# Two square roots, an exponential table, a clock and eighteen row numbers in an attention and experts kernel

## The chip, the cores and the metric

The kernel is one launch on one core of a Trainium2 chip. Its time is the device time of that launch in microseconds (us), the median of several runs. The engines are TensorE (PE in the profile, PEld for its weight loads), VectorE (DVE), ScalarE (ACT), GpSimd (POOL) and SyncE (SP, which here only issues DMAs).

## The reference

Three layers follow each other in fp32. Nothing is returned but the last.

```python
B, H, S, D = 4, 8, 576, 64
scores = where(block_i >= block_j, q @ k.T / 8, -1e9)     # blocks of 64 rows
attn = exp(scores - max); attn /= sum + 1e-9
x = (attn @ v) as rows                                    # 2304 x 512
xn = x / (norm(x) + 1e-6);  en = emb / (norm(emb) + 1e-6) # 8 experts
logits = xn @ en.T / tau                                  # tau = 0.1
expert = argmax(logits); gate = softmax(logits)[expert]
y = gate * (relu(x @ w1[expert]) @ w2[expert])            # 512 -> 1024 -> 512
h = y @ w_in;  out = (h * sigmoid(h)) @ w_out             # 512 -> 2048 -> 512
```

## The kernel before

**Stages.** Attention goes over 16 pairs (a batch and two heads each). For a pair, ScalarE or VectorE splits k and q into a high and a low part (`split`, L656), TensorE makes scores in three products (`s`), VectorE takes each row's maximum (`mx`), ScalarE makes the exponentials and their sums (`p`), TensorE transposes them (`pt`) and multiplies with v (`o`). A last small product with `rmat` turns `o` into rows of x and, in the same matmul, into the logits, for which `rmat` holds the normed expert rows (`experts`, L691, and `expert_rows`, L709). The scores of one pair come in three units: `full`, which takes both score buffers in PSUM, and two more that need a buffer back, that is, the exponentials before them. While attention runs, pieces of `w_in` are converted (`conv`, tiles `wbits`, `wcv`).

Then rows are sorted by expert into slots of 128 (`_Route`). 6 slots are filled from the first three batches (`early`), the others after the last batch (`late`, `rest`). `gates` (L1249) computes the softmax weight of each row from its logits and from `nr`, its norm, which is the root of the sum of squares `ss`. Each slot s is gathered, transposed (`xt`), multiplied by w1 (`h`), put through relu, transposed (`ht`), multiplied by w2 (`y`) and scaled by `gate` (`yout`, L1471). The last layer runs in 6 chunks of 3 slots: transposes `yt`, `up` (products `g`, then sigmoid) and `down` (products `o` into three PSUM accumulators), and `store` (L1550), which copies an accumulator out and scatters its 128 rows to `out` by an indirect DMA on GpSimd. The first chunks take their row numbers from `tokg`, the later ones read them back from DRAM with the rows (`yi`).

**Roots before.** L700 takes the root of the experts' 8 sums of squares on ScalarE; L702 is an exponential whose value nobody uses, placed behind it so that the exponential's table is loaded again. L1258 takes the root of 128x18 sums of squares on ScalarE, L1263 an exponential after it. ScalarE holds one table at a time; the instruction ACT_TABLE_LOAD changes it.

**Order of the work.** Everything between L1743 and the end is recorded in a list (`_Plan`) and put in order by a list scheduler with costs and latencies of its own. Each engine executes its instructions in the order that comes out. Work that two engines can do (copies, relus, splits) goes to the one that would finish it first by the plan (`bind`, L375), so a change of an instruction can move others. The plan takes 1283 ns for a change of table (L425) and 107 ns and more for transposes and fp32 products. The build is done four times (`_best`, L1808), each time with the due times of the one before, and the shortest plan is kept. `gates` is recorded with a priority of -1000, ahead of what stands around it. The identity matrix (L1736, L1737) is made ahead of the plan.

**Store before.** Its recorded call issues two instructions on GpSimd, a copy of 128 row numbers into a tile of their own and the scatter that reads them:

```python
eng.tensor_copy(ix, st["i"][:, a:a + 1])
ins = eng.indirect_dma_start(out, IndirectOffsetOnAxis(ap=ix, axis=0), o, None)
```

Of the kernel before, what the change touches and what calls it, by code (L numbers as in the profile page):

```python
# [9 lines left out]
F32 = mybir.dt.float32  # L10
F32R = mybir.dt.float32r
BF16 = mybir.dt.bfloat16
I32 = mybir.dt.int32
U32 = mybir.dt.uint32
AF = mybir.ActivationFunctionType
ALU = mybir.AluOpType
# [3 lines left out]
P = 128  # L20
# [8 lines left out]
NT = NTOK // P  # L29
# [8 lines left out]
PRE = 1  # L38
# [16 lines left out]
CH = 3  # L55
# [2 lines left out]
EXP_HI = 122879.9921875  # L58
NEG = -2.0 ** 100
STAY, STAY_NS, CHANGE = 30, 2000.0, 190.0  # L60
ROUNDS = 3
SQS = 100
WL = 2500.0
# [477 lines left out]
        self.free = dict.fromkeys(self.ENGINES, t)  # L541


def _column(b, tl):


    if tl == 4:
        return NC1 - 1 if b < 2 else NT - 1
    return 4 * b + tl + (b == 3)
# [52 lines left out]
def _attention(first, ctx, late, tc, plan, q, k, v, emb, tau, x_dram, identr, lr_all, ss_all, conv=None):  # L602


    nc = plan
    ident = identr.bitcast(F32)

    def pool(name, bufs, ctx=late, **kw):
        side = "left" if ctx is first else "right"
        return plan.pool(ctx.enter_context(tc.tile_pool(name=name, bufs=bufs, side=side, **kw)),  # L610
                         bufs)
# [6 lines left out]
    cp = pool("a_const", 1)  # L618
    vp = pool("a_v", 3)
    wk = pool("a_wk", 2)  # L620
    sm = pool("a_sm", 4)
    ps_t = pool("ps_t", 3, space=PSUM)
    ps_o = pool("ps_o", 1, space=PSUM)
    sp = pool("a_split", 3, ctx)
# [45 lines left out]
    load(0, "k")  # L670
    load(0, "q")


    maskq = cp.tile([P, P], F32R, name="maskq")
    maskk = cp.tile([P, 64], F32R, name="maskk")
# [15 lines left out]
    def experts():  # L691

        em = wk.tile([E, DM], F32, tag="ot", name="em")
        nc.sync.dma_start(em, emb)
        ta = cp.tile([E, 1], F32, name="ta")
        nc.sync.dma_start(ta, tau.partition_broadcast(E))
        esq = wk.tile([E, DM], F32, tag="ot", name="esq")
        en_s = cp.tile([E, 5], F32, name="en_s")
        nc.scalar.activation(esq, em, AF.Square, accum_out=en_s[:, 0:1])
        nc.scalar.activation(en_s[:, 1:2], en_s[:, 0:1], AF.Sqrt)  # L700
        if PRE:
            nc.scalar.activation(en_s[:, 4:5], en_s[:, 1:2], AF.Exp, scale=0.0)  # L702
        nc.vector.tensor_scalar(en_s[:, 2:3], en_s[:, 1:2], 1e-6, ta, ALU.add, ALU.mult)
        nc.vector.reciprocal(en_s[:, 3:4], en_s[:, 2:3])
        nc.vector.tensor_scalar_mul(esq, em, en_s[:, 3:4])
        nc.gpsimd.memset(rmat, 0.0)
        return esq
# [263 lines left out]
    for i in range(-2, NP + 2):  # L971
# [14 lines left out]
        st = s_units(i + 1) if 0 <= i + 1 < NP else []  # L986
# [15 lines left out]
class _Route:  # L1002
# [59 lines left out]
    @staticmethod  # L1062
    def bc(ap, axis, shape):
        return ap.unsqueeze(axis).to_broadcast(shape)
# [184 lines left out]
    def gates(self, pool, psum):  # L1249

        self.part = 4
        nc, V, bc = self.nc, self.nc.vector, self.bc
        self.choose(pool, NC1, NT)

        T8 = [P, NT, E]
        nr, gt = (self.tile(pool, x, [P, NT]) for x in ("nr", "gt"))
        pr = self.tile(pool, "pr", T8)
        nc.scalar.activation(nr, self.ss, AF.Sqrt)  # L1258
        V.tensor_scalar(nr, nr, 1e-6, None, ALU.add)
        V.reciprocal(nr, nr)  # L1260
        V.tensor_tensor(pr, self.lr, bc(self.mx, 2, T8), ALU.subtract)
        V.tensor_tensor(pr, pr, bc(nr, 2, T8), ALU.mult)
        nc.scalar.activation(pr, pr, AF.Exp)  # L1263
        V.tensor_reduce(gt, pr, AX.X, ALU.add)
        V.tensor_scalar(gt, gt, 1e-9, None, ALU.add)
        V.reciprocal(gt, gt)

        g3 = self.tile(pool, "g3", [P, NT, 3], BF16)
        for a in range(3):
            V.tensor_copy(g3[:, :, a], gt)  # L1270
            if a < 2:
                V.tensor_tensor(gt, gt, g3[:, :, a], ALU.subtract)
        self.g3 = g3
        self.places_of(pool, psum, "g1", self.first, NC1, 0)
# [12 lines left out]
def _layers(ctx, stage, early, scores, late, tc, plan, w1, w2, x_dram, y_dram, out, ident, route, xgs, conv, right):  # L1287

    nc = plan
# [194 lines left out]
    def chunk(c):  # L1484
        CW = CH * P
        st = {}

        def rows():
            st["y"] = yrows(c)
            if c < NC:  # L1490
                st["i"] = tokg[:, CH * c:CH * c + CH]
                return
            r0 = CW * (c - NC)
            nc.sync.dma_start(
                st["y"], y_dram[r0:r0 + CW, :].rearrange("(a p) d -> p a d", p=P))
            st["i"] = chp.tile([P, CH], I32, tag="yi", name=f"yi_{c}", bufs=2)
            nc.vector.tensor_copy(st["i"], st["y"][:, :, DM])

        def trans(kc):
            if kc == 0:  # L1500
                st["t"] = chp.tile([P, 2, KC, CW], F32R, tag="yt", name=f"yt_{c}")
            pt = psum(f"yt{kc}_{c}", "t" if c > YT else "c")
            for a in range(CH):
                nc.tensor.transpose(pt[:, a * P:(a + 1) * P],
                                    st["y"][:, a, kc * P:(kc + 1) * P], ident)
            nc.copy(st["t"][:, 0, kc], pt[:, 0:CW])
            nc.sub(st["t"][:, 1, kc], pt[:, 0:CW],
                                 st["t"][:, 0, kc].bitcast(F32))

        W = {}  # L1510

        def parts(w, f):
            if (w, f) not in W:
                if c == 0:
                    conv.piece(16 * w + f)
                W[w, f] = split((conv.win[:, f], conv.wout[:, f:f + 1, :])[w], f"w{w}_{c}_{f}")

        def up(f):
            parts(0, f)
            hi, lo = W.pop((0, f))  # L1520
            pt = psum(f"g{f}_{c}", "c")[:, 0:CW]
            t = st["t"]
            for kc in range(KC):
                nc.tensor.matmul(pt, hi[:, kc], t[:, 0, kc], start=(kc == 0), stop=False)
                nc.tensor.matmul(pt, hi[:, kc], t[:, 1, kc], start=False, stop=False)
                nc.tensor.matmul(pt, lo[:, kc], t[:, 0, kc], start=False, stop=(kc == KC - 1))
            sg = wk.tile([P, CW], F32, tag="sg", name=f"sg{f}_{c}")
            nc.scalar.activation(sg, pt, AF.Sigmoid)
            nc.vector.tensor_tensor(sg, pt, sg, ALU.mult)
            g = wk.tile([P, 2, CW], F32R, tag="g", name=f"g{f}_{c}")  # L1530
            nc.copy(g[:, 0], sg)
            nc.sub(g[:, 1], sg, g[:, 0].bitcast(F32))
            st["g", f] = g

        def down(*fs):
            if fs[0] == 0:
                st["o"] = [ps["a"].tile([P, DM], F32, tag="acc", name=f"o{a}_{c}")
                           for a in range(CH)]
            w = {}
            for f in fs:  # L1540
                parts(1, f)
                w[f] = *W.pop((1, f)), st.pop(("g", f))
            for a in range(CH):
                r = slice(a * P, a * P + P)
                for f in fs:
                    hi, lo, g = w[f]
                    three(st["o"][a], g[:, 0, r], g[:, 1, r], hi[:, 0], lo[:, 0],
                          f == 0, f == FC2 - 1)

        def store(a):  # L1550
            o = wk.tile([P, DM], F32, tag="o", name=f"os{a}_{c}", bufs=CH)
            nc.copy(o, st["o"][a])
            ix = wk.tile([P, 1], I32, tag="ix", name=f"ix{a}_{c}", bufs=CH)

            def f(eng):


                eng.tensor_copy(ix, st["i"][:, a:a + 1])  # L1558
                ins = eng.indirect_dma_start(out, IndirectOffsetOnAxis(ap=ix, axis=0), o, None)  # L1559
                for old in stores:  # L1560
                    tc.declare_no_dep(ins.ins, old.ins, reason="other rows")
                stores.append(ins)

            plan.call({"gpsimd": (f, 728.0)}, [plan._box(o), plan._box(st["i"])],
                      [plan._box(ix), (f"out_{c}_{a}", 0, 1, ((0, 1),))], dma=True)

        head = [(0.0, rows, [])] + [(0.35, lambda kc=kc: trans(kc), []) for kc in range(KC)]
        u = []
        order = [(up, 0)] + [x for f in range(1, FC2) for x in ((up, f), (down, f - 1))] + [
            (down, FC2 - 1)]  # L1570
        if c == nch - 1:

            order[-4:] = [(up, FC2 - 1), (down, FC2 - 3), (down, FC2 - 2, FC2 - 1)]
        for f, *n in order:
            u.append((1.95 * len(n), lambda f=f, n=n: f(*n),
                      [lambda f=f, m=m: parts(int(f is down), m) for m in n]))
        u += [(0.0, lambda a=a: store(a), []) for a in range(CH)]
        return head, u

# [92 lines left out]
    wk = pool("m_wk", 2)  # L1672
# [5 lines left out]
    for c in range(nch):  # L1678
# [3 lines left out]
        for at, units in ((HA, head[1:]), (HR, head[:1])):  # L1682
            i = max(n - at, 0)
            seq_c[i:i] = units
        seq_c += body
    a, c, due = early, 0, -DUE
    while a < len(seq_s) or c < len(seq_c):

        if c < len(seq_c) and a >= need[seq_c[c][0]] and (
                due <= 0 or c <= KC or a >= len(seq_s)):  # L1690
            _, w, f, _ = seq_c[c]
            c += 1
            due += w
        else:
# [4 lines left out]
            w, f = seq_s[a]  # L1699
# [108 lines left out]
def _best(build):  # L1808

    nc, plan = build(None)  # L1810
    last = plan
    for _ in range(ROUNDS):
        found, last = build(last.latest())
# [32 lines left out]
```

## Time and profile before

| what | value |
|---|---|
| median of 3 runs | 891.82 us (891.19 to 893.75) |
| the profiled execution: time of the run, span in the trace | 892.14 us, 890.4 us |
| PE, DVE, ACT, POOL busy, share of the span | 96%, 81%, 62%, 14% |
| mean granted clock of TensorE | 0.994 |
| ACT_TABLE_LOAD in the whole trace | 6, of 1283 ns |

The time of a run is 1.74 us more than the span, which goes from the first to the last instruction on the core. A busy PE is not a PE at its peak. Idle time of an engine counts only where another one waits for it.

### The profile page before, as it was taken

Reading aid. Unit: us, or ns where it says so; the run is one execution under the profiler, and the core shown is the slowest. Engines: PE = TensorE matmul, PEld = TensorE weight load, DVE = VectorE, ACT = ScalarE, POOL = GpSimd, SP = SyncE. Lnnn points to the kernel's source line nnn. Section 1 sums busy time; section 2 is a strip of 40 time slices with the busy share of each in tenths; the row PEclk is TensorE's granted clock in tenths of the full one; section 3 lists DMA queues with packets and bytes.
Section 4 is the critical chain, followed back from the end, with each engine's and each line's share of the span. In section 5 each row is a group of like instructions: output and inputs, shape, how many; then the busy total and the mean of one; then the engine's idle time right before and its main releaser. Section 6 shows DMA issues by size and latency. Waiting matters only on the chain.

```text
span 890.4 us, 13848 instructions
## 1 busy us (share of the span) xinstructions
PE 856.0 (96%) x4986; PEld 713.9 (80%) x4986; DVE 722.6 (81%) x1264; ACT 554.1 (62%) x1128; POOL 121.9 (14%) x162
## 2 busy tenths in 40 slices
PE   5999999999999999999999999999999999999995
PEld 4777677766567888888888888888999999999994
DVE  6989798988999799999888888887677767667672
ACT  7889787976467588888866665665334235334332
POOL 3013131123310000211311111002001001001001
PEclk9999999999999999999999999999999999999998
DMA  6545362473044477530102230342002002000000
GB/s 191 164 122 165 111 180 82 122 256 82 13 159 140 140 272 272 178 94 26 71 24 76 68 119 24 107 132 72 34 1 71 1 1 72 1 0 36 1 1 35
DMA packets 38440, 82.75 MB, mean 93 GB/s; under 512 B 5208, under 2 KB 13400, under 8 KB 38368
## 3 DMA queue, kind: packets, MB, share of 16 engines
q1 hardware_dynamic: 32736, 63.47, 22.2%
q0 software_dynamic: 5632, 18.36, 6.7%
q8 instruction: 40, 0.66, 0.3%
q14 instruction: 32, 0.26, 0.1%
HBM read 123.23 MB, written 13.11 MB: 153 GB/s over the span
## 4 chain that ended last, share of the span: by engine, by line
PE 65%; POOL 0%; POOLq 0%; issue 0%; ACT 0%
PE o L199 22%; PE g L199 22%; PE y L199 9%; PE h L199 9%; PE ht L199 2%; PE xt L199 1%; PE yt L199 1%; POOL out_dram L1559 0%; POOLq L1838 0%; ACT os L199 0%; POOL ix L1558 0%; POOLq L1559 0%
## 5 line engine op out<-in xcount | busy, mean ns | idle before, releaser
L199 PE MATMUL o<-w,g 128*128 128x512 f32 x864 | 234.2, 396 | 0.0
L199 PE MATMUL g<-yt,w 128*128 128x384 f32 x1152 | 230.7, 337 | 0.0
L199 PEld LDWEIGHTS g<-yt,w 128*128 128x128 f32 x1152 | 203.9, 188 | 13.8
L199 PEld LDWEIGHTS o<-w,g 128*128 128x128 f32 x864 | 160.0, 188 | 27.4 <-ACT g L199 0.3
L199 ACT ACTIVATE sg<-g 128x384 f32<-128x384 f32 x96 | 47.4, 494 | 141.9 <-PE g L199 141.8
L199 PE MATMUL y<-w2s,ht 128*128 128x512 f32 x450 | 131.3, 402 | 1.2 <-DVE w2s L199 1.2
L199 PE MATMUL h<-w1s,xt 128*128 128x512 f32 x450 | 110.4, 394 | 3.4 <-DVE xt L199 2.0
L199 PEld LDWEIGHTS h<-w1s,xt 128*128 128x128 f32 x450 | 83.5, 188 | 22.1 <-ACT h L199 2.0
L199 DVE TENSOR_TENSOR w1s<-wraw,w1s 128x1024 fp32r<-128x1024 f32 x75 | 91.2, 1221 | 11.4 <-ACT w1s L199 11.1
L199 DVE TENSOR_TENSOR w2s<-wraw,w2s 128x1024 fp32r<-128x1024 f32 x75 | 91.0, 1224 | 10.0 <-ACT w2s L199 8.7
L199 PEld LDWEIGHTS y<-w2s,ht 128*128 128x128 f32 x450 | 81.2, 188 | 16.3 <-DVE w2s L199 2.7
L199 ACT ACTIVATE p<-s,mx 128x576 f32<-128x576 f32 (+4 forms) x160 | 82.7, 527 | 15.7 <-DVE mx L199 12.9
L199 DVE TENSOR_TENSOR w<-win,w 128x512 fp32r<-128x512 f32 x96 | 66.0, 689 | 24.0 <-ACT w L199 23.4
L199 ACT CAST w2s<-wraw 128x1024 fp32r<-128x1024 f32 x68 | 71.0, 1051 | 14.2 <-PE h L199 7.4
L199 ACT CAST g<-sg 128x384 fp32r<-128x384 f32 x96 | 49.4, 514 | 39.9 <-DVE sg L199 38.3
L258 PE MATMUL s<-ks,qs 64*128 64x288 f32 (+4 forms) x576 | 61.3, 344 | 13.1 <-ACT p L199 7.7
L199 DVE TENSOR_REDUCE mx<-s 128x1 f32<-128x576 f32 (+3 forms) x96 | 64.6, 705 | 10.5 <-PE s L258 9.5
L199 ACT CAST w1s<-wraw 128x1024 fp32r<-128x1024 f32 x53 | 55.6, 1054 | 20.7 <-PE y L199 15.2
L199 DVE TENSOR_TENSOR w<-wout,w 128x512 fp32r<-128x512 f32 x96 | 65.6, 683 | 0.2 <-ACT w L199 0.2
L199 ACT CAST w<-win 128x512 fp32r<-128x512 f32 x75 | 46.6, 625 | 28.7 <-PE o L199 28.6
L258 PEld LDWEIGHTS s<-ks,qs 64*128 64x128 f32 x576 | 46.5, 199 | 20.0 <-ACT p L199 10.5
L199 DVE TENSOR_TENSOR sg<-g,sg 128x384 f32<-128x384 f32 x96 | 53.3, 556 | 10.6 <-ACT sg L199 7.9
(194 smaller groups left out, 1127.5 us busy)
## 6 DMA issues: line engine op xcount, KB each, us to landing
wraw<-in_moe_w_dram SPq DMA_DIRECT2D x76, 1024.0 KB
wbits<-in_moe_w_in_dram SPq DMA_DIRECT2D x16, 512.0 KB
wbits<-in_moe_w_out_dram SPq DMA_DIRECT2D x16, 512.0 KB
k<-in_k_dram SPq DMA_DIRECT2D x16, 288.0 KB
q<-in_q_dram SPq DMA_DIRECT2D x16, 288.0 KB
v<-in_v_dram SPq DMA_DIRECT2D x16, 256.0 KB
x_rows<-xe POOLq DMA_DIRECT2D x16, 256.0 KB, 4.1
wraw<-in_moe_w_dram SPq DMA_DIRECT2D x8, 512.0 KB
```

Source lines behind the costliest of these rows:

```text
L199: alts = {e: (lambda eng, m=m, a=a, k=k: getattr(eng, m)(*a, **k), self._cost(e, m, a, k), self._shares(e, m, a, k) if e != "tensor" else ...
L258: eng.matmul(out, a, b, **kw)
```

## The change

The root on ScalarE is replaced at both places by a start value from the bits of the number (a shift and an addition) and three steps of Heron on VectorE, each a reciprocal and two scalar_tensor_tensor operations; the steps leave twice the root, and a factor of 0.5 goes into the addition of 1e-6. The exponential at L702 goes. A new exponential of one column of zeros and 14 fp32 products of the identity with itself, whose result nobody reads, stand behind the loads of the first k and q. The copies of row numbers are recorded at the start of a chunk's `down` work, each into its own tile, and the call of a store issues the scatter and behind it a copy of the row numbers into a tile that nobody reads.

```diff
+GROOT, WARM = 1, 14
+def _root(V, z, t, x):
+    zi, xi = z.bitcast(I32), x.bitcast(I32)
+    V.tensor_scalar(zi, xi, 1, None, ALU.logical_shift_right)
+    V.tensor_scalar(zi, zi, float(0x20400000), None, ALU.add)
+    for _ in range(3):
+        V.reciprocal(t, z)
+        V.scalar_tensor_tensor(t, t, 2.0, x, ALU.mult, ALU.mult)
+        V.scalar_tensor_tensor(z, z, 0.5, t, ALU.mult, ALU.add)
...
     load(0, "k")
     load(0, "q")
+    one = cp.tile([P, 1], F32, name="one")
+    nc.vector.memset(one, 0.0)
+    nc.scalar.activation(one, one, AF.Exp)
+    pt = ps_t.tile([P, 512], F32, tag="t", name="t_warm")
+    for _ in range(WARM):
+        nc.tensor.matmul(pt[:, 0:P], ident, ident, start=True, stop=True)
...
-        nc.scalar.activation(en_s[:, 1:2], en_s[:, 0:1], AF.Sqrt)
-        if PRE:
-            nc.scalar.activation(en_s[:, 4:5], en_s[:, 1:2], AF.Exp, scale=0.0)
-        nc.vector.tensor_scalar(en_s[:, 2:3], en_s[:, 1:2], 1e-6, ta, ALU.add, ALU.mult)
+        _root(nc.vector, en_s[:, 1:2], en_s[:, 4:5], en_s[:, 0:1])
+        nc.vector.tensor_scalar(en_s[:, 2:3], en_s[:, 1:2], 0.5, 1e-6, ALU.mult, ALU.add)
+        nc.vector.tensor_tensor(en_s[:, 2:3], en_s[:, 2:3], ta, ALU.mult)
...
-        nc.scalar.activation(nr, self.ss, AF.Sqrt)
-        V.tensor_scalar(nr, nr, 1e-6, None, ALU.add)
+        if GROOT:
+            _root(V, nr, nt, self.ss)
+            V.tensor_scalar(nr, nr, 0.5, 1e-6, ALU.mult, ALU.add)
...
             if fs[0] == 0:
+                st["ix"] = [wk.tile([P, 1], I32, tag="ix", name=f"ix{a}_{c}", bufs=CH)
+                            for a in range(CH)]
+                for a in range(CH):
+                    nc.gpsimd.tensor_copy(st["ix"][a], st["i"][:, a:a + 1])
...
-                eng.tensor_copy(ix, st["i"][:, a:a + 1])
                 ins = eng.indirect_dma_start(out, IndirectOffsetOnAxis(ap=ix, axis=0), o, None)
...
+                eng.tensor_copy(spare, ix)
```

## Rows read from the trace of the kernel before

**Rows 1.** Windows: stretch, length, busy of PE, PEld, DVE, ACT, POOL, clock, DMA, GB/s.

```profile
10.00:15.00 5.00, 4.08 (x30) 3.80 (x30) 2.14 (x6) 4.32 (x10) 2.19 (x8) 1.00 0.56 170
...
40.00:60.00 20.00, 19.92 (x195) 15.84 (x192) 18.37 (x42) 15.74 (x46) 2.40 (x2) 1.00 0.37 112
...
220.00:240.00 20.00, 17.86 (x81) 11.26 (x80) 18.65 (x55) 8.39 (x13) 2.93 (x2) 1.00 0.05 14
...
270.00:280.00 10.00, 10.00 (x52) 8.55 (x51) 9.76 (x15) 9.12 (x13) 0.00 (x0) 1.00 0.46 159
```

**Rows 2.** Timeline, ACT to 11 us: start, length, engine, instruction, idle before.

```profile
0.81 1.28 ACT L199 ACT_TABLE_LOAD   x1 [0.81 <-PEq L1832]
...
6.45 0.67 ACT L199 CAST ks<-k 128x576 fp32r<-128x576 f32 x1 [0.62 <-DMA k<-in_k_dram]
...
7.14 1.28 ACT L199 ACT_TABLE_LOAD   x1
...
8.66 1.28 ACT L199 ACT_TABLE_LOAD   x1
...
10.06 0.72 ACT L199 ACTIVATE p<-s,mx 128x576 f32<-128x576 f32 x1
```

**Rows 3.** Timeline, DVE and PE of the same stretch.

```profile
1.42 0.65 DVE L1737 CAST ident<-xg 128x128 fp32r<-128x128 f32 x1 [1.42 <-POOL xg masks.py:199]
...
5.27 1.33 PE L258 MATMUL s<-ks,qs 64*128 64x288 f32 x8 [5.27 <-ACT qs L199]
...
6.47 0.83 PE L258 MATMUL s<-ks,qs 64*128 64x288 f32 x4
...
7.46 0.46 DVE L199 TENSOR_SCALAR qs<-q 128x576 fp32r<-128x576 f32 x1 [1.40 <-DMA q<-in_q_dram]
...
8.51 1.42 DVE L199 TENSOR_REDUCE mx<-s 128x1 f32<-128x576 f32 x2
...
10.92 1.12 PE L258 MATMUL s<-ks,qs 64*128 64x448 f32 x4 [3.63 <-ACT p L199]
```

**Rows 4.** Timeline of PE at three later places, and one window.

```profile
18.80 1.09 PE L199 MATMUL pt<-ident,p 128*128 128x128 f32 x4 [0.25 <-DVE pt L199]
...
29.69 1.53 PE L199 MATMUL pt<-ident,p 128*128 128x128 f32 x12
...
188.26 0.67 PE L258 MATMUL s<-ks,qs 64*128 64x448 f32 x4 [1.41 <-ACT p L199]
```

**Rows 5.** Window of PE: stretch, length, busy, clock, DMA, GB/s.

```profile
188.00:192.00 4.00, 3.74 (x45) 0.77 0.74 278
```

**Rows 6.** Timeline around the gates.

```profile
214.40 0.22 ACT L199 ACTIVATE r_nr<-ss 128x18 f32<-128x18 f32 x1
...
218.62 3.01 PE L199 MATMUL h<-w1s,xt 128*128 128x512 f32 x12 [1.79 <-DVE xt L199]
219.59 0.17 DVE L199 TENSOR_SCALAR r_nr<-r_nr 128x18 f32<-128x18 f32 x1
...
222.68 0.30 DVE L199 TENSOR_REDUCE r_gt<-r_pr 128x18 f32<-128x144 f32 x1
...
224.02 0.17 DVE L199 TENSOR_SCALAR r_gt<-r_gt 128x18 f32<-128x18 f32 x1
224.10 0.17 DVE L199 TENSOR_SCALAR c_cnt<-r_run 128x8 f32<-128x8 f32 x1
...
227.92 0.18 DVE L199 CAST r_g<-r_gt 128x18 bf16<-128x18 f32 x1
...
231.93 0.16 DVE L199 TENSOR_TENSOR gate<-gate,g 128x6 f32<-128x6 f32 x1
```

**Rows 7.** Timeline of POOL at the end.

```profile
880.70 0.98 POOL L1559 DMA_INDIRECT out_dram<-os,ix  x1 [60.04 <-ACT os L199]
881.69 0.19 POOL L1558 COPY ix<-yi 128x1 int32<-128x1 int32 x1
882.16 0.98 POOL L1559 DMA_INDIRECT out_dram<-os,ix  x1 [0.28 <-POOL ix L1558]
```

More of the change, by code (lines that the diff above doesn't have):

```diff
@@ L1255, in gates @@
         T8 = [P, NT, E]
-        nr, gt = (self.tile(pool, x, [P, NT]) for x in ("nr", "gt"))
+        nr, gt, nt = (self.tile(pool, x, [P, NT]) for x in ("nr", "gt", "nt"))
         pr = self.tile(pool, "pr", T8)
-        nc.scalar.activation(nr, self.ss, AF.Sqrt)
-        V.tensor_scalar(nr, nr, 1e-6, None, ALU.add)
+        if GROOT:
+            _root(V, nr, nt, self.ss)
+            V.tensor_scalar(nr, nr, 0.5, 1e-6, ALU.mult, ALU.add)
+        else:
+            nc.scalar.activation(nr, self.ss, AF.Sqrt)
+            V.tensor_scalar(nr, nr, 1e-6, None, ALU.add)
         V.reciprocal(nr, nr)
@@ L1552, in store @@
             nc.copy(o, st["o"][a])
-            ix = wk.tile([P, 1], I32, tag="ix", name=f"ix{a}_{c}", bufs=CH)
+            ix = st["ix"][a]
+            spare = wk.tile([P, 1], I32, tag="spare", name=f"sp{a}_{c}", bufs=CH)
             def f(eng):
-                eng.tensor_copy(ix, st["i"][:, a:a + 1])
                 ins = eng.indirect_dma_start(out, IndirectOffsetOnAxis(ap=ix, axis=0), o, None)
@@ L1562, in f @@
                 stores.append(ins)
-            plan.call({"gpsimd": (f, 728.0)}, [plan._box(o), plan._box(st["i"])],
-                      [plan._box(ix), (f"out_{c}_{a}", 0, 1, ((0, 1),))], dma=True)
+                eng.tensor_copy(spare, ix)
+            plan.call({"gpsimd": (f, 728.0)}, [plan._box(o), plan._box(ix)],
+                      [plan._box(spare), (f"out_{c}_{a}", 0, 1, ((0, 1),))], dma=True)
         head = [(0.0, rows, [])] + [(0.35, lambda kc=kc: trans(kc), []) for kc in range(KC)]
```

## The prediction

> **What bounds the kernel now.** I read the windows first. PE is busy 19.92 of 20 us at 40 to 60 and all of 270 to 280, while VectorE stands at 18.37 of 20 and 9.76 of 10 [rows 1]. So the body is bound by TensorE with VectorE close behind; a delay of either reaches the end there, and time taken from ScalarE reaches it only where somebody waits for ScalarE. The windows name the exceptions. From 10 to 15 us PE has 4.08 of 5 us, and at 220 to 240 it has 17.86 of 20 while VectorE has 18.65 and ScalarE only 8.39 [rows 1]. Three places matter for this change, and for each I read the timeline.
>
> At the start PE finishes the first scores at 6.47 + 0.83 = 7.30 and then sits idle 3.63 us until 10.92, released by ScalarE's first `p` [rows 3]. ScalarE ends `ks` at 6.45 + 0.67 = 7.12, loads a table at 7.14, another at 8.66, and starts `p` at 10.06 [rows 2]: 2.94 us that hold two loads of 1.28 and two tiny activations. But `p` also needs a row maximum. The two `mx` began only at 8.51, since VectorE first did the q split of the next pair, for which it had waited 1.40 us on a DMA [rows 3]. One reduction is 1.42 / 2 = 0.71, so the first was there at 9.22.
>
> Around the gates, the products `h` at 218.62 waited 1.79 us for VectorE's `xt` split [rows 6]. ScalarE's root, at 214.40, was long done, and VectorE came to its result only at 219.59 [rows 6].
>
> At the end POOL alone sets the pace: scatter 0.98 at 880.70, copy at 881.69, 0.28 of waiting, scatter at 882.16 [rows 7]. The next copy and scatter repeat this; nothing else runs.
>
> **The change part by part.** The sum is made against the profiled execution, 892.14 us, which is a span of 890.4 and 1.74 around it. The median of the three runs is 891.82, 0.32 lower.
>
> *The start.* Gone are two loads, a root and a dummy exponential, 2.94 us of ScalarE ahead of the first `p`. The new exponential's load takes the place of the load at 0.81 [rows 2], which lies ahead of the arrival of k, so it costs nothing; uncovered it would cost 1.28. What is late next is `mx`. If VectorE keeps its order, `p` starts about 0.1 behind 9.22: a gain of 10.06 - 9.35 = 0.7. If the scheduler, which no longer sees two loads of 1283 ns between the scores and `p`, puts `mx` first, then VectorE was idle (the 1.40 before 7.46) and `mx` starts some 0.2 after the scores end, at 7.5; `p` follows at 7.5 + 0.71 + 0.1 = 8.3, a gain of 1.75. I take 1.75: the reduction is then the only thing between two products on the engine that bounds everything, and the split serves a later pair. Ends: 2.94 gained at best. On the other side about 14 new VectorE operations for the experts' root come in here. The nearest, on 18 columns, starts 0.08 behind its predecessor and lasts 0.17 [rows 6]; 14 x 0.17 = 2.4 if all stood in front of `mx`, of which 1.40 finds VectorE idle, so a loss of 1.0 less the 0.7: 0.3 lost at worst. The next engine downstream is PE, nearly full from here on, so the gain is carried on to the end.
>
> *The 14 products.* The trace has no fp32 product of the identity; the nearest rows are transposes of the same shape, 4 in 1.09 us at 18.80 and 12 in 1.53 at 29.69 [rows 4], 0.27 and 0.13 each: the lower and the upper of the two clock levels (1.2 and 2.4 GHz), though no granted clock below 1.00 is recorded there. The identity is ready at 1.42 + 0.65 = 2.07 [rows 3]. 14 of them end between 2.07 + 1.8 = 3.9 and 2.07 + 3.8 = 5.9; the scores began at 5.27. So they cost 0 to 0.6, and if the clock is then up, the 12 score products save up to half of their 2.03 us, 1.0. I take zero, since the low parts of q are not there before about 6.1 anyway. Does the higher level last until the second scores? A later stretch says no: after PE had idled 1.41 us at 188.26 [rows 4], the granted clock of 188 to 192 averages 0.77 [rows 5], that is, part of it stood at the lower level. The gap here will be about 2 us. The Trainium skill says the same of idle stretches in "TensorE: Matmul & The Clock Gate", under "What's actually happening", and it is the rule that speaks against this edit; the fourth case below is what happens if it is wrong here.
>
> *The gates.* Gone are two loads and a root, 2.78 us of ScalarE, in a stretch where ScalarE idles more than half [rows 1]: nothing by itself. Added are 11 small operations on VectorE (13 for root and addition of 1e-6 and the reciprocal, where 2 were). They lie beside large ones; 224.02 and 224.10 start 0.08 apart [rows 6], so I take 0.1 each, 1.1 us, in a stretch that VectorE bounds. Against it stands that a relu or a cast of 0.7 to 1.0 may go to the freed ScalarE. I take a net loss of 0.4. Ends: 11 x 0.17 plus waiting of 0.06 each, 2.5 lost; two casts moved, 1.5 gained. By the Trainium skill, "VectorE: DVE Perf Modes", "The DRAIN you can't avoid", the next operation does not start until the pipe is empty, which would make it 11 x 0.17 = 1.9 lost and the sum 1.5 worse in that term; the two starts 0.08 apart speak against it here.
>
> *The stores.* The copies move to the start of `down`, where POOL, busy for 14% of the span, hides them; behind them in POOL's queue are only gathers and scatters of rows that are planned ahead. The first scatter waited 60.04 us on ScalarE, not on its copy [rows 7], so nothing is gained there. The second and third lose the wait of 0.28 but keep a copy of 0.19 before them, the one into `spare`. 2 x 0.28 = 0.56. Ends: 0 if the 0.28 is what an indirect DMA needs to start, 0.94 if the copy is overlapped too. I take 0.5.
>
> *Everything else.* No DMA is added or moved past another, but the scheduler lays the whole order anew. I put nothing for that, with an estimated 1.5 us to either side: PE's idle time at 220 to 240 alone is 2.14 us [rows 1], and a new order may find or lose about that.
>
> Sum: -1.75 + 0.4 - 0.5 = -1.85, 890.3 by the profiled execution's own time and 890.0 against the median. I predict 889.9.
>
> **The rivals.** *Order at the start unchanged.* VectorE still does the next pair's split before `mx`: -0.7, and the gates cost their full 1.1, the stores give 0.3. Sum +0.1: 891.9. For it: that split was also ahead when nothing forced it. Against: it was ahead while 2.57 us of loads covered it.
>
> *The gate comes late (slower).* The root is a chain of 11 links, and each has to wait for the one before it while large operations are let in between. The seven links from 222.68 to 227.92 took 5.24 us, 0.75 each [rows 6]. 11 x 0.75 = 8.2 us; before, 219.59 - 214.62 = 5.0 us lay between the end of the root on ScalarE and the addition. The gate, at 231.93, would come 3.2 us later, and if larger operations of 1.2 us slip between the links, 6. Slot 0's PSUM bank is held until it is scaled, so PE stalls for what goes beyond about half a microsecond of slack. It decides from a gate later than about 234.5: 6 - 0.5 = 5.5 lost, less 2.2 from start and stores: 895.1. Against it: the chain can start 5 us earlier than the addition did, in slots that exist already.
>
> *The clock stays up.* If the level reached by the 14 products outlasts the gap, the products from 10.92 to about 22 run at twice the rate. PE was busy 4.08 of 5 us there [rows 1], so some 9 of 11 us, 4.5 at most; ScalarE's exponentials are nearly as full (4.32 of 5), so I give it half, 2.3 more: 887.6.
>
> *It changes nothing.* PE's loss at the start is refilled by what waits on the loads of later pairs, the gates and the new order eat the rest. This falls at 891.8, beside the first rival.
>
> **How the numbers follow.** The likeliest, 889.9, has 0.42 and a range of its own of 888.4 to 891.4. Order unchanged or nothing: 0.23. Late gate: 0.11. Clock up: 0.20. What I have not thought of, evenly to both sides: 0.04. The range of 8 in 10 goes from 886.6, a clock that stays up with a full gain of ScalarE's 2.94, to 893.9, the gates' upper bound with the first rival. About 0.3%, 2.7 us, is what a measurement of this kernel can tell from no change, so faster means below 889.1: 0.18 of the clock's 0.20, 0.16 of the likeliest, 0.03 elsewhere, 0.37. Slower means above 894.5: 0.09 of the late gate, 0.03 elsewhere, 0.12. The rest, 0.51, lies between.
>
> **What would show it.** Two ACT_TABLE_LOAD in the whole trace, one before k and one before the first sigmoid. `p` first starts between 8 and 8.6 (9.3 if the order stays), and the second scores before 9.4. The 14 products end between 3.9 and 5.9, and the first 8 scores take less than 1.33 us; the transposes behind them are still at about 0.27 each (0.13 if the clock stayed). The 11 links at the gates start about 0.1 before their successors, the gate is there by 233 less the start's gain, and the wait of 1.79 on `xt` is not longer. The last scatter starts about 0.5 us sooner after the last product. I am wrong if `p` moves up and the span doesn't, if the gate moves past 234.5, or if PE's idle time between 30 and 300 us changes by more than the start gives.

## The result, and the profile after

The changed kernel took 902.1 us (median of 4 runs, 900.9 to 903.9) against 892.1 before: ratio 1.0111 [1.0087, 1.0136], 10 us slower where I had forecast 2 us faster. 902.1 lies outside my range. The profiled execution took 902.8, span 901.1, so the 10.7 us by which its span is longer can be looked for in the trace. One execution of e5 below took 1095.6 us at a mean granted clock of 0.734, and its figures leave it out.

Busy time and count of each engine, first part of the page:

```profile
PE 864.4 (96%) x5014; PEld 719.1 (80%) x5014; DVE 723.9 (80%) x1281; ACT 556.5 (62%) x1131; POOL 125.4 (14%) x178
```

Windows of the changed kernel (columns as in [rows 1]), with the stretches of [rows 1, 5]:

```profile
10.00:15.00 5.00, 3.55 (x36) 2.68 (x36) 4.42 (x13) 5.00 (x16) 1.66 (x4) 1.00 0.74 212
15.00:20.00 5.00, 3.55 (x21) 2.71 (x22) 3.19 (x11) 4.21 (x13) 1.80 (x1) 0.66 0.62 160
20.00:25.00 5.00, 4.23 (x27) 3.58 (x29) 4.17 (x16) 2.04 (x5) 0.00 (x0) 0.50 0.65 204
25.00:30.00 5.00, 5.00 (x32) 4.67 (x30) 3.67 (x7) 2.93 (x10) 0.00 (x0) 0.50 0.01 3
40.00:60.00 20.00, 19.85 (x173) 14.58 (x174) 18.29 (x38) 16.50 (x53) 2.59 (x2) 1.00 0.36 114
188.00:192.00 4.00, 3.54 (x35) 2.49 (x32) 3.26 (x20) 3.35 (x14) 0.59 (x1) 1.00 0.00 2
220.00:240.00 20.00, 18.57 (x67) 10.93 (x67) 17.79 (x52) 11.08 (x21) 5.04 (x5) 1.00 0.30 73
270.00:280.00 10.00, 8.95 (x40) 5.63 (x40) 9.27 (x17) 8.42 (x15) 1.38 (x1) 1.00 0.50 171
```

The body is no longer full: 8.95 of 10 at 270 to 280, where before had 10.00. From 20 to 30 us the granted clock is 0.50, the lower level, 1.2 GHz.

The start, ScalarE (answers to [rows 2]):

```profile
0.80 1.28 ACT L200 ACT_TABLE_LOAD   x1 [0.80 <-PEq L1859]
...
6.12 0.67 ACT L200 CAST ks<-k 128x576 fp32r<-128x576 f32 x1 [0.36 <-DMA k<-in_k_dram]
...
9.46 0.74 ACT L200 ACTIVATE p<-s,mx 128x576 f32<-128x576 f32 x1 [0.49 <-DVE mx L200]
```

VectorE and PE of the same stretch (answers to [rows 3, 4]):

```profile
2.12 5.42 PE L200 MATMUL t_warm<-ident 128*128 128x128 f32 x28 [2.12 <-DVE maskq L200]
7.47 0.80 PE L259 MATMUL s<-ks,qs 64*128 64x288 f32 x8
...
8.67 1.42 DVE L200 TENSOR_REDUCE mx<-s 128x1 f32<-128x576 f32 x2 [1.03 <-PE s L259]
...
10.34 0.68 PE L259 MATMUL s<-ks,qs 64*128 64x448 f32 x4 [1.71 <-ACT p L200]
...
16.89 1.11 PE L200 MATMUL pt<-ident,p 128*128 128x128 f32 x4 [0.47 <-ACT p L200]
17.93 1.33 PE L259 MATMUL s<-ks,qs 64*128 64x288 f32 x8
...
21.46 0.47 DVE L200 TENSOR_SCALAR esq<-em,en_s 8x512 f32<-8x512 f32 x1
...
22.07 0.56 PE L200 MATMUL t_en<-ident,esq 8*128 8x8 f32 x4 [0.77 <-DVE pt L200]
```

The loads are gone and `mx` is put ahead of the next pair's q split, as forecast. The 14 products are 28 records and end at 7.54, 2.27 behind the time at which the scores began before. The scores then take 0.80 where they took 1.33, `p` comes 0.60 sooner and the second pair's scores 1.88 sooner (17.93 against 19.81). At 16.89 four transposes take 1.11 again: the lower level is back, after waits of 0.91, 0.18, 1.00 and 0.47 us between the transposes.

From there the gain turns round. I took the start of the same work in both traces: each pair's first scores, each slot's first transposes `xt`, each chunk's first transposes `yt`. Changed minus before, us: second pair -1.88, third +2.31, sixth +4.08, last +6.88, slot 0 +10.00, slot 2 +9.52, first `yt` +11.17, last `yt` +11.16. The last `yt` is 131.25 us ahead of the last product in both. So nearly all is lost by the first `yt`, at 276.8 us: 6.9 of it by the last pair of attention, which no edit touches except at its start, and 3.1 more up to slot 0.

The waits there, between 34 and 200 us (waiter <- releaser: total, times, longest). Before:

```profile
ACT p L199 <- DVE mx L199: 12.3, 13, 2.1
...
DVE mx L199 <- PE s L258: 6.2, 11, 0.9
```

Changed:

```profile
ACT p L200 <- DVE mx L200: 19.1, 21, 1.9
...
DVE mx L200 <- PE s L259: 12.2, 16, 2.6
```

There are 37 such waits where 24 were: all along attention, maxima and exponentials wait more for what stands before them.

The gates (answers to [rows 6]):

```profile
222.79 0.21 DVE L200 TENSOR_SCALAR r_nr<-ss 128x18 int32<-128x18 int32 x1 [1.41 <-ACT sqs L200]
...
226.87 3.15 PE L200 MATMUL h<-w1s,xt 128*128 128x512 f32 x12 [0.57 <-DVE xt L200]
...
235.48 0.17 DVE L200 TENSOR_SCALAR r_nr<-r_nr 128x18 f32<-128x18 f32 x1
...
243.38 0.34 DVE L200 TENSOR_TENSOR gate<-gate,g 128x6 f32<-128x6 f32 x2
...
243.75 0.69 ACT L200 ACTIVATE yr<-y,gate 128x512 f32<-128x512 f32 x1 [1.35 <-DVE gate L200]
...
244.97 0.93 PE L200 MATMUL h<-w1s,xt 128*128 128x512 f32 x2 [1.47 <-ACT xt L200]
```

The root and the addition behind it stretch from 222.79 to 235.48 between larger operations; `yr` waits 1.35 for the gate, ScalarE's cast of `xt` stands behind `yr`, and PE waits 1.47 for that cast.

The end of POOL (answers to [rows 7]):

```profile
891.35 0.99 POOL L1585 DMA_INDIRECT out_dram<-os,ix  x1 [58.28 <-ACT os L200]
892.34 0.19 POOL L1589 COPY sp<-ix 128x1 int32<-128x1 int32 x1
892.69 0.99 POOL L1585 DMA_INDIRECT out_dram<-os,ix  x1 [0.16 <-issue]
```

Scatters are 1.34 apart instead of 1.46. From the last product to the end of the span it is 8.75 us, 9.27 before.

### The profile page after: what moved, and what is told of

Its sections match the earlier page's. It is cut to its first block, busy times and chain, and to the rows that moved or that the text cites. A ratio compares the mean times of both kernels' runs of the same rounds, so it can differ in the third digit from the quotient of the medians.

```text
span 901.1 us, 13945 instructions
## 1 busy us (share of the span) xinstructions
PE 864.4 (96%) x5014; PEld 719.1 (80%) x5014; DVE 723.9 (80%) x1281; ACT 556.5 (62%) x1131; POOL 125.4 (14%) x178
## 4 chain that ended last, share of the span: by engine, by line
PE 64%; issue 0%; POOL 0%; ACT 0%; POOLq 0%
PE o L200 22%; PE g L200 21%; PE y L200 9%; PE h L200 9%; PE ht L200 1%; PE xt L200 1%; PE yt L200 1%; POOL out_dram L1585 0%; ACT os L200 0%; POOL sp L1589 0%; POOLq L1865 0%
## 5 line engine op out<-in xcount | busy, mean ns | idle before, releaser
L200 DVE TENSOR_TENSOR w2s<-wraw,w2s 128x1024 fp32r<-128x1024 f32 x75 | 91.3, 1224 | 11.6 <-ACT w2s L200 10.2
L200 ACT ACTIVATE p<-s,mx 64x64 f32<-64x64 f32 (+4 forms) x160 | 82.6, 526 | 23.7 <-DVE mx L200 23.1
L200 ACT CAST w2s<-wraw 128x1024 fp32r<-128x1024 f32 x71 | 74.6, 1052 | 17.1 <-PE h L200 8.9
L200 DVE TENSOR_REDUCE mx<-s 128x1 f32<-128x576 f32 (+4 forms) x96 | 65.2, 706 | 19.9 <-PE s L259 17.3
L200 ACT CAST w1s<-wraw 128x1024 fp32r<-128x1024 f32 x56 | 58.9, 1054 | 22.2 <-PE y L200 16.9
L200 PE MATMUL pt<-ident,p 128*128 128x128 f32 (+1 forms) x400 | 61.8, 288 | 6.9 <-ACT p L200 2.6
L200 ACT CAST w<-win 128x512 fp32r<-128x512 f32 x81 | 50.5, 625 | 26.1 <-PE o L200 25.8
```

The lines of the kernel that those rows point to most:

```text
L200: alts = {e: (lambda eng, m=m, a=a, k=k: getattr(eng, m)(*a, **k), self._cost(e, m, a, k), self._shares(e, m, a, k) if e != "tensor" else ...
```

## The experiments

Theory A: the order that the scheduler lays anew costs the time, the edits hardly any. Theory B: the edits cost it where they stand. Each set was timed in turns with the kernel before on one chip (before: 892.3, 892.7 and 893.3 in the three sets).

**e1: the old order, all edits.** Each changed call is planned as the call of before and issued as the new one; the new exponential and the 14 products, which had no call before, are issued ahead of the plan. For the gates' root:

```
+ _stand_in(nc, "scalar", "activation", (nr, self.ss, AF.Sqrt), {},
+           lambda: _root(nc.nc.vector, nr, nt, self.ss), AF.Sqrt)
```

> All four edits, but the scheduler plans the calls of the kernel before, so that every other instruction stands on its engine in the order of before. Theory A (the new order costs the time, the edits hardly any): 889 to 892.5 us, the first p starts near 9.4 as in the changed kernel and the attention stage keeps the spacing of before. Theory B (the edits cost it themselves: 14 products of 5.42 us that hold up the first scores until 7.47, roots on VectorE): 898 to 903 us.

Measured: 894.8, ratio 1.0028 [1.0018, 1.0039]: between the two ranges.

**e2: the changed kernel's order, none of its instructions.** The same device the other way round: planned as the new calls, issued as the old ones. For the gates (`_Silent` plans each call of the root and issues the one old call at the first of them):

```
- _root(V, nr, nt, self.ss)
+ _root(_Silent(nc, lambda: nc.nc.scalar.activation(nr, self.ss, AF.Sqrt)), nr, nt, self.ss)
```

> The scheduler plans the calls of the changed kernel, but the instructions issued are those of before (roots and both table loads on ScalarE, no products of the identity, row numbers copied beside the stores). Theory A: 897 to 903 us, with none of the edits in it. Theory B: 891 to 893.5 us.

Measured: 902.4, 1.0118 [1.0103, 1.0132]. The order alone is as slow as the whole change.

**e3: the kernel before, with two orders of its scheduler to choose from instead of four.**

```
- ROUNDS = 3
+ ROUNDS = 1
```

> The kernel before with ROUNDS = 1: two plans are made instead of four and the shorter kept, whose length by the scheduler's own costs is 877.8 us, against 872.4 for the plan of before and 877.5 for that of the changed kernel. No instruction is changed, the order alone. Theory A: 895 to 900 us, about the 5.4 us of the plans' difference. Theory B: within 1.5 us of 892.

Measured: 902.7, 1.0122 [1.0107, 1.0137], above A's range too.

**e4: e1 without the 14 products.**

```
- for _ in range(14):
-     tc.nc.tensor.matmul(wt[:, 0:P], ident, ident, start=True, stop=True)
```

> As the first run, without the 14 products. Theory A: 888.5 to 891.5 us, within 2 us of the first run: the first scores start at 5.3 and p near 9.3. Theory B with the products as the cause: at least 5 us below the first run.

Measured: 896.3, 1.0046 [1.0033, 1.0059]. By e2 and e3 the order costs about 10 us with no edit in the kernel, so B falls as the main cause. But e1 and e4 are above A's ranges: edits that I took for nearly free cost 2.5 in the old order. By the medians the products are worth 1.6 (e4 less e1), though the two intervals overlap.

In e1's trace, the loss stood between the slots 1 and 2 (`xt` +0.15, then +3.74). That gave the second set.

**e5: the old order, the gates' root alone** (the two lines of e1; everything else is the kernel before).

> The order of the kernel before; of the change only the gates' root is in (11 operations in a row on VectorE where ScalarE's root was planned, ScalarE's two table loads there gone). Theory G (the whole price of the edits in the old order is this one: the row of 11 stands in front of the relu of the slot's second half, PE idles behind it and then runs its next 12 products at the lower clock level): 895.5 to 896.5, that is 3.4 to 4.0 above before, all of it between the second and the third slot. Rival P (my prediction's term, 0.4 lost, or nothing, and the 3.7 us seen at that place come with the other edits): 891.5 to 893.

Measured: 896.2, 1.0035 [1.0022, 1.0048]: theory G. Timeline of e5, VectorE and PE:

```profile
215.19 0.16 DVE L547 TENSOR_SCALAR r_nr<-ss 128x18 int32<-128x18 int32 x1
...
217.76 0.69 DVE L199 TENSOR_SCALAR h<-h 128x512 f32<-128x512 f32 x1
...
218.51 0.66 PE L199 MATMUL ht<-ident,h 128*128 128x128 f32 x4 [1.52 <-DVE h L199]
...
221.66 5.41 PE L199 MATMUL h<-w1s,xt 128*128 128x512 f32 x12 [2.50 <-DVE xt L199]
```

And its window of 221 to 227 (columns as in [rows 1]):

```profile
221.00:227.00 6.00, 5.33 (x13) 4.27 (x14) 6.00 (x12) 0.32 (x1) 0.00 (x0) 0.51 0.00 0
```

11 operations in a row take 2.57 us in front of the relu. PE waits 1.52 for the relu and 2.50 for `xt`, and then the 12 products take 5.41 where they took 3.01 [rows 6], at a granted clock of 0.51. A delay of 2.57 is thus paid nearly twice, 2.6 + 2.4; some 1.2 come back, since the `w2s` for which the next products waited before is ready by then. The lag goes from +0.60 at slot 1 to +4.24 at slot 2.

**e6: the old order, all edits but the gates' root.**

```
- _stand_in(nc, "scalar", "activation", (nr, self.ss, AF.Sqrt), {},
-           lambda: _root(nc.nc.vector, nr, nt, self.ss), AF.Sqrt)
...
+ nc.scalar.activation(nr, self.ss, AF.Sqrt)
```

> The order of the kernel before with three edits in: the experts' root, exponential's table with the 14 products, and the row numbers. Theory G: e1 less the gate's price, 894.8 - 3.7 = 891.1, so 890.3 to 892.0: about 1 below before. Rival P (the gate's root costs little and the loss comes with the other edits): 893.5 to 895.

Measured: 891.3, 0.9986 [0.9977, 0.9996], the one version that beats both kernels; it is 1.2 us below before. Timeline of its PE:

```profile
2.12 5.62 PE L701 MATMUL t_warm<-ident 128*128 128x128 f32 x28 [2.12 <-DVE maskq L199]
7.67 0.79 PE L258 MATMUL s<-ks,qs 64*128 64x288 f32 x8
...
11.09 1.08 PE L258 MATMUL s<-ks,qs 64*128 64x448 f32 x12
...
17.17 1.33 PE L258 MATMUL s<-ks,qs 64*128 64x288 f32 x8
...
250.10 5.52 PE L199 MATMUL h<-w1s,xt 128*128 128x512 f32 x18
```

The second pair comes 2.64 sooner, and this gain stands unchanged through all 16 pairs and up to slot 3 (-2.75): in this order a gain at the start is carried on. At slot 4 it is -1.31: the 18 products at 250.10 took 5.52 where those of before took 4.35, and a window of that stretch shows the lower level:

```profile
250.00:253.00 3.00, 3.00 (x14) 2.44 (x12) 1.47 (x6) 0.47 (x1) 0.08 (x1) 0.57 0.94 356
```

**e7: e6 with 6 products, and the experts' root behind the first row maxima.**

```
- for _ in range(14):
+ for _ in range(6):
...
  def scaled():        # issued where `en_s` was scaled before
+     _root(V, en_s[:, 1:2], en_s[:, 4:5], en_s[:, 0:1])
```

> The order of the kernel before, no root for the gates, 6 products in place of 14, the experts' root issued behind the first pair's row maxima instead of ahead of them, exponential's table and the row numbers as in the change. Theory: 6 products are 12 passes at some 0.2 us, over at about 4.7, before the scores want PE; nothing stands ahead of the row maxima, so p of the first pair starts at 9.4 to 9.9 (10.06 before), and the gain of 1.0 that the variant without products kept through all pairs stays or grows; with 0.2 to 0.7 of the stores that is 889.8 to 891.2. Rival (the start's gain is lost again before the slots, as in the changed kernel): 891.8 to 893.

Measured: 893.7, 1.0010 [1.0001, 1.0019]: above both ranges, and as the rival has it the start gains nothing (third pair +0.62). Its trace:

```profile
5.04 1.32 PE L258 MATMUL s<-ks,qs 64*128 64x288 f32 x8
...
10.41 0.13 DVE L547 TENSOR_SCALAR en_s<-en_s 8x1 int32<-8x1 int32 x1
...
14.70 2.46 DVE L199 TENSOR_REDUCE mx<-s 128x2 f32<-128x896 f32 x4
...
16.07 0.63 ACT L199 ACTIVATE p<-s,mx 128x448 f32<-128x448 f32 x1 [2.39 <-DVE mx L199]
```

After 6 products (12 records) the first scores still take 1.32, and the row of small operations, moved from a place where VectorE waited for q to one where it had work, put `mx` of the second round to 14.70 (13.14 before). The two edits of e7 were not separated.

**e8, e11 and e12: other orders of the kernel before**, by one constant of its scheduler; e11 and e12 change the price of a change of mode in the same way.

```
- STAY, STAY_NS, CHANGE = 30, 2000.0, 190.0
+ STAY, STAY_NS, CHANGE = 30, 1800.0, 190.0
```

> The kernel before, no edit in it, with one constant of its scheduler changed (how long an engine's mode is worth staying in, 1800 instead of 2000): the order is another, and by the scheduler's own costs as long as the one before (872.8 against 872.4; the changed kernel's is 877.5 and the one with two builds 877.8, both measured 10 us longer). Theory L (the scheduler's length tells the time: 10 us measured for 5 planned): 892 to 894.5. Rival K (its costs don't tell, and the order of before is a rare good one): 897 to 903.

> The kernel before, no edit, price of a change of mode 204: planned 873.3, against 872.4 of before and 872.8 of the order that took 898.7. Theory D: 895 to 903, so that before's 892 stands below its neighbours. Rival (the order at 898.7 was an outlier and planned lengths near 872 mean 892): 891.5 to 894.

> The kernel before, no edit, price of a change of mode 196: planned 875.8, half a us from the two drawn orders of the changed kernel. Theory D: 896 to 903, no different from them. Rival E: 2.5 or more below both of them.

**e9 and e10: two more orders of the changed kernel.** For e10:

```
- LATENCY = {"tensor": 195.0, "vector": 128.0, "scalar": 190.0, ...}
+ LATENCY = {"tensor": 195.0, "vector": 128.0, "scalar": 194.0, ...}
```

> The changed kernel, all edits as they are, with the scheduler's price of a change of mode at 164 instead of 190, so that it lays another order (876.3 by its own costs; the changed kernel's is 877.5). Theory D (the order is a draw: each one that the scheduler finds is some us longer or shorter whatever the edits, and before has the good one): 896 to 903, about where the orders without edits lie (898.7 and 902.7 so far). Rival E (the edits make every order worse than its like without them, by their own 2.5 on top): 901 to 906, above both drawn orders of the kernel before.

> The changed kernel again, with the latency that the scheduler assumes of ScalarE at 194 instead of 190: a third order, also 876.3 by its own costs. Theory D: 896 to 903, not the same time as the order before it although the planned length is the same. Rival E: 901 to 906. If the planned length told the time, both would be equal within 1 us and about 2 below the changed kernel, 900.

All orders together, with the scheduler's own length of each, and the lag behind before (profiled executions, us) at the third pair, the last pair, slot 0 and the first `yt`:

| order | planned | median | ratio | 3rd pair | last pair | slot 0 | first `yt` |
|---|---|---|---|---|---|---|---|
| before | 872.4 | 892.3 to 893.3 | 1 | 0 | 0 | 0 | 0 |
| e12, no edits | 875.8 | 896.9 | 1.0047 [1.0029, 1.0064] | +0.5 | +1.2 | +3.2 | +1.8 |
| e8, no edits | 872.8 | 898.7 | 1.0064 [1.0048, 1.0080] | +1.1 | +0.7 | +9.6 | +6.9 |
| e11, no edits | 873.3 | 898.8 | 1.0064 [1.0048, 1.0079] | +0.8 | +4.4 | +6.8 | +7.0 |
| e3, no edits | 877.8 | 902.7 | 1.0122 [1.0107, 1.0137] | +3.8 | +4.3 | +9.7 | +7.0 |
| changed | 877.5 | 902.1 | 1.0111 [1.0087, 1.0136] | +2.3 | +6.9 | +10.0 | +11.2 |
| e9, changed | 876.3 | 901.4 | 1.0098 [1.0083, 1.0114] | +2.4 | +4.4 | +6.7 | +9.2 |
| e10, changed | 876.3 | 903.9 | 1.0111 [1.0090, 1.0131] | +4.2 | +8.6 | +10.2 | +16.2 |

The profiled execution of e12 was its shortest and that of e10 its longest, so their lags stand some 3 and 4 us off the medians. e8 fell in the range of K, e11 in that of D, e9 in those of D and E, e10 in that of E alone.

Theory D holds in its main point: each of the four other orders of the unedited kernel is 4 to 11 us slower than the one it has, and none of the seven other orders, with edits or without, reaches it. Wherever an edit made the scheduler lay a new order, this one was given up. The planned length tells the time in part: the three orders of 872.8 to 875.8 took 896.9 to 898.8, the four of 876.3 to 877.8 took 901.4 to 903.9. But 872.4 and 872.8 are 6 us apart on the chip. Each order loses at other places, ahead of the first `yt` but for some 2 us of e3.

Rival E is neither shown nor refuted. For it, e12 came out as E said and not as D did, 4.5 and 7 us below e9 and e10; and the mean ratio is 1.0074 for the four orders without edits and 1.0107 for the three with them, 3 us apart and near the 2.5 of e1. Against it, the edited orders are also longer by plan, e3 lies above e9, and in the one order that was timed both ways the edits make no difference (e2 902.4, the changed kernel 902.1). What makes the order of before good I can't say; that stays open. Its scheduler's constants may have been set by measuring, which no run here can tell.

## Why the prediction was wrong

**The step that failed** is "Everything else: ... the scheduler lays the whole order anew. I put nothing for that, with an estimated 1.5 us to either side". In its place the runs show +10 (e2: that order with the old instructions), and +4 to +11 for four other orders without edits. I took the bound from PE's idle time at 220 to 240 alone, 2.14 us, the time that a new order could find or lose in one stretch. But an order is laid for the whole kernel. From 30 to 300 us PE was idle for 14.3 us before and for 19.3 in the changed kernel (19.9 in e2): 5.1 lost in small waits, besides the 2.3 by which the third pair was late. The granted clock averages 0.99 over that stretch in both, so it explains little; the other 4 of the 11.2 were not traced. Nor were the two sides alike: all seven other orders are slower. Two figures that need no run pointed that way. The changed kernel's planned length, 877.5, is 5.1 above that of before, and the scheduler's four rounds for the kernel before have planned lengths of 890.4, 877.8, 881.4 and 872.4, a spread of 18 that one window could not show. Two of the prediction's own signs of being wrong came with it: `p` moved up and the span didn't, and PE's idle time from 30 to 300 us changed by more than the start gave.

**The start, -1.75:** right in size to the second pair (-1.88) by luck, for it came another way. `p` came at 9.46, not 8 to 8.6, since `mx` waited 1.03 us for scores that the products held back; the gain came from scores at twice the rate. It was gone a pair later: against e2, which has this order without the edits, the second pair is 2.15 sooner and the third 0.43. `esq` came at 21.46 (16.39 before), as the links of the experts' root stand between larger operations, and the clock had fallen: 0.66, then 0.50 to 30 us. e2 has about the same lag at the third pair (+2.7) with no edit in it, so the order alone does as much. In the old order the third pair is 2.6 sooner in e6's profiled execution and 0.45 later in e1's, though the two issue the same up to there; what the start is worth there depends on the clock of the execution (last section).

**The 14 products, 0 to 0.6:** mis-sized. I counted 14 rows; 28 ran, and ended at 7.54, not by 5.9. In the profiled executions of the changed kernel and e6 the scores and transposes to about 16 us then run at the higher level, which pays for it; in that of e1 only the first scores do. So the 1.6 by which e1 is below e4 is not shown to come from this. The rival of the clock that stays up held to about 16 us and no further. The Trainium skill ("TensorE: Matmul & The Clock Gate", "What's actually happening") says that an idle PE loses its clock; e5 (0.51 after waits of 1.52 and 2.50) and the stretch from 15 us on (0.66, then 0.50, after waits of 0.91, 0.18, 1.00 and 0.47) agree with it.

**The gates, +0.4 (at worst 2.5):** +3.5 in the old order (e5), outside both ends, because I priced the row of operations but not the clock that PE loses while it waits. In the changed kernel, where the scheduler spread the links, the lag did not grow from slot 0 to slot 2 (+10.00, +9.52); it grew by 1.7 to the first `yt` (+11.17). That looks like the rival of the late gate: the gate comes at 243.7, PE waits 1.47, and the products behind take 5.12 for 16. But e2, with the old root in the same order, shows the same; timeline of its ScalarE and PE:

```profile
242.46 0.69 ACT L200 ACTIVATE yr<-y,gate 128x512 f32<-128x512 f32 x1 [1.02 <-DVE gate L200]
...
243.68 0.72 PE L200 MATMUL h<-w1s,xt 128*128 128x512 f32 x2 [1.57 <-ACT xt L200]
244.83 5.38 PE L200 MATMUL h<-w1s,xt 128*128 128x512 f32 x16 [0.43 <-DVE xt L200]
```

So this wait belongs to the order, and no run shows a loss by the root there. The rival's half a microsecond of slack stands in no row, and 243.7 is past its 234.5 only because the whole stage is 10 late.

In a row, a link took 2.57 / 11 = 0.23, not 0.1: the two starts 0.08 apart on which I leaned belong to operations that don't wait for each other. The same timeline has operations on `r_gt` that do, 0.20 and 0.30 apart (the first at 224.02 [rows 6]):

```profile
224.22 0.27 DVE L199 RECIPROCAL r_gt<-r_gt 128x18 f32<-128x18 f32 x1
...
224.52 0.19 DVE L199 CAST r_g<-r_gt 128x18 bf16<-128x18 f32 x1
```

So the rule that I set aside, of the Trainium skill's "VectorE: DVE Perf Modes", "The DRAIN you can't avoid", has the right side for such a row: in e5 each link starts 0.03 behind the end of the one before. The two starts 0.08 apart, at a length of 0.17, go against it, and no run separates an empty pipe from the dependence as the reason.

**The stores, -0.5:** 8.75 against 9.27 from the last product to the end, 0.52 gained in the changed kernel. In e1, e4 and e6 it is 9.24 to 9.25: the closer scatters gain 0.24 there, and the last copy into `spare`, which now ends the queue, takes 0.2 back. In the changed kernel and e9, but not in e10 (9.25), the first scatter also starts 0.5 sooner, 0.28 behind the end of the first `os` instead of 0.29 behind that of the second; why only there stays open.

**Table loads:** two in the whole trace, at 0.80 and 288.36, as forecast.

**Slips of the working** that change nothing: the sum gives 890.0, not 889.9; the gates' upper bound with the first rival gives 893.3, not 893.9; the raised clock with the full 2.94 gives 886.4, not 886.6; and the experts' root adds 12 operations and a memset, not 14.

## What to carry to other kernels

Where a scheduler lays the order of the whole kernel, an edit of a few instructions is two changes, the edit and a new draw of the order; issue the edit in the old order to time the first, and lay other orders of the unedited kernel to size the second, before the edit's own terms are argued about. Here the terms were 0.2 to 4 us and the draw 4 to 11. A row of dependent small operations on VectorE costs little where that engine waits for a load (e6), and more than its length, 3.5 for 2.57, where PE waits for the engine and loses its clock (e5).

## What the runs showed of the hardware that I had not expected

- A product of the identity with itself in fp32 leaves two records on PE: 28 for 14, 12 for 6.
- The clock at the start differs between executions of the same instructions. Up to the gates e1 and e6 issue the same; the 28 records took 6.17 in e1 and 5.62 in e6, and 12 of the second scores 1.90 and 1.08, so the second pair came at 19.73 and 17.17. Timeline of PE in e1, and one of its windows:

```profile
2.12 6.17 PE L701 MATMUL t_warm<-ident 128*128 128x128 f32 x28 [2.12 <-DVE maskq L199]
...
11.82 1.90 PE L258 MATMUL s<-ks,qs 64*128 64x448 f32 x12
```

```profile
12.00:14.00 2.00, 2.00 (x19) 1.96 (x19) 0.93 (x1) 2.00 (x4) 1.03 (x1) 0.50 0.49 152
```

- The clock column does not show every slow product: before, it reads 1.00 from 5 to 8 us, and the first 8 scores take 1.33 [rows 3]; in e6 it reads 1.00 too, and they take 0.79.
- A scatter starts 0.16 behind a copy that it does not need, and 0.28 behind one that it does [rows 7].
